# q and k as pairs of 16-bit floats, and P V as one key chunk in every step

## The chip, the core and the metric

The program runs on one core of a Trainium2 chip. The metric is the device time of one execution in microseconds. The kernel before was run three times: 1413.3, 1413.76 and 1414.07 us, so its median is 1413.76 us.

TensorE does the matrix products, VectorE, ScalarE and GpSimd the work on elements, and SyncE issues most of the transfers. Each of them has its own queue of instructions that it works through in order.

## The reference

An attention layer is followed by a top-1 mixture of experts:

```python
q_pool = q.reshape(B, H, S // 2, 2, D).mean(axis=3)          # 8 x 8 heads, 1152 -> 576 queries, D = 64
scores = scale * np.matmul(q_pool, k.transpose(0, 1, 3, 2))  # 576 x 1152 of each head
scores = scores - np.max(scores, axis=-1, keepdims=True)
attn = np.exp(scores)
attn = attn / (np.sum(attn, axis=-1, keepdims=True) + 1e-09)
attn_out = np.matmul(attn, v)
# then for each of 4608 tokens: one of 8 experts, relu(x W1) W2, times a gate
```

All inputs are float32, and the result is held to float32 accuracy. So the kernel splits each operand into a high and a low part and multiplies the parts.

## The kernel before

The attention works on 32 pairs of heads, one after the other. A pair has 18 steps: 9 chunks of 128 keys for the first head, then 9 for the second. In each step (`scores`, L349 to L390) TensorE makes the scores of one chunk of 128 keys against all 576 queries: two matmuls of 288 columns with the stacked high and low parts of q (L361) and two with the low part of k and a row of maxima (L363). The operands are float32 values of reduced precision (`F32R`): `ka` holds the high part of k twice, `kb` the low part and a row of -1, `qa` the high and low parts of q, `qb` the high part of q and the row maxima. The scores land in one of two tiles of PSUM, `sps0` for the even steps and `sps1` for the odd ones.

Then the weights P = exp(scores) are split into `ph` and `pl`, both of 16 bits. In the steps listed in `PLP` (the odd steps 1 to 15) ScalarE writes `ph` (L377), writes the exact exponential back over the scores in PSUM (L378), and VectorE takes the difference (L381); only then is the score tile free for the step after the next. In all other steps ScalarE writes the exponential to memory (L385) and as `ph` (L386), which frees the score tile, and GpSimd takes the difference (L387). The last pair does the same with other steps (`PLPL`).

Beside this, TensorE makes the scores of the next pair with queries on the partitions (L300: three tiles of 384 columns for every two steps, two of them in an odd step and one in an even one, with one or two matmuls each), and VectorE reduces each to a maximum (L301). After nine rows of them a small transpose, a subtraction (L340) and a transfer put the maxima into `qb`. P V (`av`, L396 to L419) takes one chunk of 128 keys at a time: 5 blocks of queries times three matmuls of 64 or 65 columns (L402 to L404), 15 in all. `BURST` says how many chunks are taken in which step, counted from 6 steps after the scores: two in nearly each even step, none in an odd one. After nine chunks the rows are normalised on VectorE (L411 to L413). A router on the finished heads (L452 to L464 and on) adds a few transposes and small matmuls in even steps.

The operands of a pair are made some 30 steps ahead by the entries of the table `PREP`: two transfers bring q and k; ScalarE casts k to its high part in two halves (`kh`, L227) and q (`qh`, L236); GpSimd adds the two queries of a pooled pair (`qsum`, L233) and makes the low parts of k (`kl`, L230) and q (`ql`, L239); transfers from memory to memory (`dmaf`, L126) lay the parts out in `ka`, `kb`, `qa`, `qb`. v has `lv`, `vh` (L259), `vs` (L263) and `vl` (L266). The order of the instructions on TensorE, VectorE, ScalarE and GpSimd is the order of the code. In each step that is: the differences left from the step before, the routers, the scores and their exponentials, `PREP`, the tiles of maxima, `BURST`, `PREP`.

After the attention come the experts, whose weights (`raw1a`, `raw2a`, `raw1b`, `raw2b`) are loaded by SyncE into memory that the attention's tiles had held: the pools of both stages are laid over each other from the same address on.

## Time and profile before

| | us |
|---|---|
| median of three runs | 1413.76 |
| the profiled execution | 1414.16 |
| its span, first to last instruction | 1412.4 |
| scores of step 0 to those of the last step | about 25 to 925 |

The profiled execution took 1414.16 us, of which 1412.4 us lie between its first and its last instruction. All times below are microseconds from the start of the span unless they are marked ns. A group of instructions is given with its count, its busy time, the mean of one in ns, and the idle time of the engine just before them with what ended it. Matmuls are pipelined: a row of one lasts from its start until its last result is there, so the distance of two starts tells what one costs in a row of many, and the duration of the last one tells when the results can be read. The same holds for ScalarE and VectorE, where the next instruction starts some 0.1 us before the one ahead of it has ended.

### The profile page before, as it was taken

The numbers are of one execution on the slowest core, as the hardware profiler recorded it, in microseconds if no ns is written. First come the engines' busy times: TensorE is split into PE (matmuls) and PEld (weight loads), VectorE is DVE, ScalarE is ACT, GpSimd is POOL, SyncE is SP. The second block draws the span as 40 slices with busy tenths as digits, with TensorE's granted clock in tenths as the row PEclk, the third lists the DMA queues.
The fourth block names the chain that finished last, engine by engine and source line by source line (L and its number), as shares of the span: only waits on it lengthen the run. The fifth ranks groups of instructions, "written<-read, shape, count | busy, mean of one in ns | idle before, by whom it ended". The sixth has DMA issues, their size and how long they took to land.

```text
span 1412.4 us, 38742 instructions
## 1 busy us (share of the span) xinstructions
PE 1345.4 (95%) x15024; PEld 1210.1 (86%) x15024; DVE 1080.5 (77%) x2153; ACT 1088.4 (77%) x1906; POOL 919.6 (65%) x768
## 2 busy tenths in 40 slices
...
PEclk9999999999999999999999999999999999999999
...
GB/s 180 163 191 206 145 186 175 165 169 172 178 157 174 168 178 185 140 176 203 163 137 203 139 191 112 154 170 259 325 241 226 294 239 278 235 280 225 322 240 47
...
## 3 DMA queue, kind: packets, MB, share of 16 engines
...
q8 instruction: 122, 2.00, 0.6%
...
q14 instruction: 69, 0.57, 0.1%
HBM read 169.47 MB, written 22.50 MB: 136 GB/s over the span
## 4 chain that ended last, share of the span: by engine, by line
PE 65%; DVE 18%; ACT 9%; issue 5%; DMA 1%; POOL 1%; ACTq 0%; DVEq 0%; POOLq 0%; SPq 0%
PE hps L918 14%; PE sps L361 10%; PE mp L300 7%; PE sps L363 7%; DVE pl L381 7%; DVE pm L301 5%; PE yp L972 4%; PE yp L973 4%; PE yp L975 4%; ACT sps L378 3%; PE av L402 3%; PE av L404 3%; PE av L403 3%; ACT ph L377 2%; DVE xb L413 1%
## 5 line engine op out<-in xcount | busy, mean ns | idle before, releaser
L301 DVE TENSOR_REDUCE pm<-mp 128x1 f32<-128x384 f32 x864 | 450.5, 550 | 146.6 <-PE mp L300 146.6
L387 POOL TENSOR_TENSOR pl<-p,ph 128x576 f16<-128x576 f32 x324 | 415.4, 1286 | 152.0 <-ACT ph L386 108.1
L361 PE MATMUL sps<-qa,ka 128*128 128x288 f32 x1152 | 282.4, 326 | 34.3 <-DVE pl L381 27.6
L402 PE MATMUL av<-vt,ph 128*128 128x65 f16 x2880 | 295.9, 194 | 0.0
L403 PE MATMUL av<-vt,ph 128*128 128x64 f16 x2880 | 293.9, 194 | 0.0
L404 PE MATMUL av<-vt,pl 128*128 128x65 f16 x2880 | 293.0, 192 | 0.0
L402 PEld LDWEIGHTS <-ph 128*128 128x128 f16 x2880 | 262.5, 97 | 28.2 <-issue 5.0
L300 PE MATMUL mp<-ka,qa 128*128 128x384 f32 x960 | 270.0, 345 | 2.0 <-DVE pm L301 1.7
L403 PEld LDWEIGHTS <-ph 128*128 128x128 f16 x2880 | 265.7, 97 | 0.7
L404 PEld LDWEIGHTS <-pl 128*128 128x128 f16 x2880 | 266.1, 99 | 0.0
L363 PE MATMUL sps<-qb,kb 65*128 65x288 f32 x1152 | 247.5, 297 | 0.0
L385 ACT ACTIVATE p<-sps 128x576 f32<-128x576 f32 x324 | 211.4, 653 | 33.2 <-PE sps L363 32.3
L377 ACT ACTIVATE ph<-sps 128x576 f16<-128x576 f32 x248 | 162.4, 655 | 96.7 <-PE sps L363 82.7
L361 PEld LDWEIGHTS sps<-qa,ka 128*128 128x128 f32 x1152 | 182.3, 190 | 49.7 <-PE av L404 25.2
L381 DVE TENSOR_TENSOR pl<-sps,ph 128x576 f16<-128x576 f32 x248 | 187.9, 758 | 35.8 <-ACT sps L378 30.6
L386 ACT ACTIVATE ph<-sps 128x576 f16<-128x576 f32 x324 | 211.7, 654 | 0.0
L918 PE MATMUL hps<-x,w1h 128*128 128x512 f32 (+1 forms) x608 | 201.5, 391 | 5.4 <-DVE x L899 5.2
L363 PEld LDWEIGHTS sps<-qb,kb 65*128 65x128 f32 x1152 | 187.0, 190 | 0.0
L300 PEld LDWEIGHTS mp<-ka,qa 128*128 128x128 f32 x960 | 163.6, 189 | 13.3 <-DVE pm L301 12.8
L378 ACT ACTIVATE sps<-sps 128x576 f32<-128x576 f32 x248 | 161.7, 652 | 0.0
L918 PE MATMUL hps<-x,w1l 128*128 128x256 f32 (+1 forms) x608 | 143.6, 277 | 0.0
L945 ACT COPY hs<-hps 128x512 f32<-128x512 f32 (+1 forms) x76 | 43.0, 565 | 128.1 <-PE hps L918 120.4
...
## 6 DMA issues: line engine op xcount, KB each, us to landing
...
```

The source lines that it names most:

```text
L300: nc.tensor.matmul(mp, lhsT=l, rhs=r, start=j == 0, stop=j == len(ops) - 1)
L301: nc.vector.tensor_reduce(out=pm[:, i:i + 1], in_=mp, axis=AX.X, op=ALU.max)
L361: nc.tensor.matmul(sps[:, j, 0:288], lhsT=ka[:, h, ks], rhs=qa[:, o + 288 * j:o + 288 * j + 288], start=True, stop=False)
L363: nc.tensor.matmul(sps[:, j, 0:288], lhsT=kb[:, h, ks], rhs=qb[:, h, 288 * j:288 * j + 288], start=False, stop=True)
L381: nc.vector.tensor_tensor(out=pl.rearrange("p (j n) -> p j n", j=2), in0=x, in1=ph2, op=ALU.subtract)
L385: nc.scalar.activation(out=p32.rearrange("p (j n) -> p j n", j=2), in_=x, func=AF.Exp, scale=1.0 / 16)
L386: e_ = nc.scalar.activation(out=ph2, in_=x, func=AF.Exp, scale=1.0 / 16)
L387: nc.gpsimd.tensor_tensor(out=pl, in0=p32, in1=ph, op=ALU.subtract)
L402: nc.tensor.matmul(av_[:, qb, 0:65], lhsT=hi, rhs=vt[:, h, c, 0:65], start=c == 0 and qb == 0, stop=False)
L403: nc.tensor.matmul(av_[:, qb, 0:64], lhsT=hi, rhs=vt[:, h, c, 66:130], start=False, stop=False)
L404: nc.tensor.matmul(av_[:, qb, 0:65], lhsT=lo, rhs=vt[:, h, c, 0:65], start=False, stop=c == NC - 1 and qb == 4)
L918: d['mm'] = nc.tensor.matmul(hp[:, f, 0:n], lhsT=W1[l][g][:, c, fs], rhs=d['x'][:, c, 0:n], start=c == 0 and l == 0, stop=c == 3 and l == 0)
```

## The change

The parts of q and k become 16-bit floats (`F16`), so that the tiles `ka`, `kb`, `qa`, `qb`, `kp`, `xk`, `xq`, `yq` have half the bytes. k is multiplied by 4096 before it is split, on ScalarE as the scale of the cast (`kh` is now an ACTIVATE), and on GpSimd by a new instruction `ks` ahead of `kl`; the exponentials divide by 4096 again through their scale. The row of -1 becomes -32768, and the row maxima are divided by 32768. `qs` gets a tile of its own. In `PREP` the entry `ks` stands at 17 and `kl` moves from 18 to 20. `BURST` becomes one chunk in each of the 18 steps. `PLP` gets the step 17.

```diff
-PREP = ((0, 'lk'), (12, 'kh', 0), (12, 'qsum'), (17, 'kh', 1), (18, 'kl'), (18, 'dk', 0), ...
+PREP = ((0, 'lk'), (12, 'kh', 0), (12, 'qsum'), (17, 'kh', 1), (17, 'ks'), (20, 'kl'), (18, 'dk', 0), ...
-BURST = {0: 2, 2: 2, 4: 2, 6: 2, 8: 1, 10: 2, 12: 2, 14: 2, 16: 3}
-PLP = (1, 3, 5, 7, 9, 11, 13, 15)
+BURST = {i: 1 for i in range(18)}
+PLP = (1, 3, 5, 7, 9, 11, 13, 15, 17)
+KS, KR = 2.0 ** 12, 2.0 ** 15
...
-                L[i] = (lp if i == order[2] else ep).tile(shape, F32R, name=f"{name}{i}")
+                L[i] = (lp if i == order[2] else ep).tile(shape, F16, name=f"{name}{i}")
...
-        nc.vector.memset(KBs[0].bitcast(F32)[64:65], -1.0)
+        nc.vector.memset(KBs[0][64:65], -KR)
...
             def kh(i):
                 z = slice(i * NQ, i * NQ + NQ)
-                nc.scalar.copy(out=xk[:, z], in_=kpf[:, z])
+                nc.scalar.activation(out=xk[:, z], in_=kpf[:, z], func=AF.Copy, scale=KS)
+
+            def ks():
+                nc.gpsimd.tensor_scalar(out=kpf, in0=kpf, scalar1=KS, scalar2=1.0, op0=ALU.mult, op1=ALU.mult)
 
             def kl():
-                nc.gpsimd.tensor_tensor(out=kp, in0=kpf, in1=xk.bitcast(F32), op=ALU.subtract)
+                nc.gpsimd.tensor_tensor(out=kp, in0=kpf, in1=xk, op=ALU.subtract)
...
-                    nc.vector.tensor_scalar(out=mr, in0=tp, scalar1=c0, scalar2=None, op0=ALU.subtract)
+                    nc.vector.tensor_scalar(out=mr, in0=tp, scalar1=c0, scalar2=1.0 / KR, op0=ALU.subtract, op1=ALU.mult)
...
-                    nc.scalar.activation(out=ph2, in_=x, func=AF.Exp, scale=1.0 / 16)
-                    e_ = nc.scalar.activation(out=x, in_=x, func=AF.Exp, scale=1.0 / 16)
+                    nc.scalar.activation(out=ph2, in_=x, func=AF.Exp, scale=1.0 / 16 / KS)
+                    e_ = nc.scalar.activation(out=x, in_=x, func=AF.Exp, scale=1.0 / 16 / KS)
```

TensorE, an odd step of pair 11 and what follows it, before (`sps11` the scores, `mp12` the tiles of maxima of the next pair, `tp` a transpose of the router, `av11` P V):

```order
L361 MATMUL sps11_7444<-qa2_125,ka2_122 128x288 x2
L363 MATMUL sps11_7444<-qb2_128,kb2_119 128x288 x2
L300 MATMUL mp12_7454<-ka0_123,qa0_126 128x384
L300 MATMUL mp12_7459<-ka0_123,qa0_126 128x384
L452 MATMUL tp_7463<-ident_64,xb_5498 128x128 x2
L361 MATMUL sps11_7469<-qa2_125,ka2_122 128x288 x2
L363 MATMUL sps11_7469<-qb2_128,kb2_119 128x288 x2
L300 MATMUL mp12_7478<-ka0_123,qa0_126 128x384 x2
L402 LDWEIGHTS ph_7249
L402 MATMUL av11_7410<-vt1_137,ph_7249 128x65
```

The same place now, from the last matmul of the odd step's scores on (line numbers are 4 higher):

```order
L367 LDWEIGHTS kb2_119
L367 MATMUL sps11_7445<-qb2_128,kb2_119 128x288
L304 LDWEIGHTS qa0_126
L304 MATMUL mp12_7454<-ka0_123,qa0_126 128x384
L304 LDWEIGHTS qa0_126
L304 MATMUL mp12_7459<-ka0_123,qa0_126 128x384
L406 LDWEIGHTS ph_7238
L406 MATMUL av11_7424<-vt1_137,ph_7238 128x65
L407 LDWEIGHTS ph_7238
L407 MATMUL av11_7424<-vt1_137,ph_7238 128x64
L408 LDWEIGHTS pl_7239
L408 MATMUL av11_7424<-vt1_137,pl_7239 128x65
```

Fifteen matmuls of P V have moved between the odd step's tiles of maxima and the scores of the even step, and each matmul on 16-bit operands has a weight load as an instruction of its own.

VectorE, from the difference of step 15 of pair 11 to that of step 1 of pair 12, before (`pl` the difference, `pm` the maxima of one tile, `m9` those of a row):

```order
L381 TENSOR_TENSOR pl_7717<-sps11_7718,ph_7716 128x576
L301 TENSOR_REDUCE pm_7555<-mp12_7744 128x1
L301 TENSOR_REDUCE pm_7555<-mp12_7789 128x1
L301 TENSOR_REDUCE pm_7555<-mp12_7792 128x1
L308 TENSOR_REDUCE m9_7795<-pm_7555 128x4
L301 TENSOR_REDUCE pm_7809<-mp13_7810 128x1
L301 TENSOR_REDUCE pm_7809<-mp13_7861 128x1
L301 TENSOR_REDUCE pm_7809<-mp13_7864 128x1
L381 TENSOR_TENSOR pl_7844<-sps12_7845,ph_7843 128x576
```

And now:

```order
L385 TENSOR_TENSOR pl_7733<-sps11_7734,ph_7732 128x576
L305 TENSOR_REDUCE pm_7571<-mp12_7776 128x1
L305 TENSOR_REDUCE pm_7571<-mp12_7803 128x1
L305 TENSOR_REDUCE pm_7571<-mp12_7806 128x1
L385 TENSOR_TENSOR pl_7795<-sps11_7796,ph_7794 128x576
L312 TENSOR_REDUCE m9_7809<-pm_7571 128x4
L305 TENSOR_REDUCE pm_7839<-mp13_7840 128x1
L305 TENSOR_REDUCE pm_7839<-mp13_7877 128x1
L305 TENSOR_REDUCE pm_7839<-mp13_7880 128x1
L385 TENSOR_TENSOR pl_7859<-sps12_7860,ph_7858 128x576
```

A ninth difference, that of step 17, stands on VectorE in each pair, and GpSimd has one fewer.

GpSimd, where the operands of pair 13 are made during pair 11, before (`kp13` the low part of k, `yq` the sum and then the low part of q):

```order
L233 TENSOR_TENSOR yq_7238<-qp_7235 128x576
L387 TENSOR_TENSOR pl_7397<-p32_7403,ph_7396 128x576
L230 TENSOR_TENSOR kp13_7233<-kpf_7234,xk13_7237 128x1152
L387 TENSOR_TENSOR pl_7468<-p32_7474,ph_7467 128x576
L239 TENSOR_TENSOR yq_7238<-yq_7238,xq_7239 128x576
```

And now:

```order
L237 TENSOR_TENSOR qs_7252<-qp_7249 128x576
L391 TENSOR_TENSOR pl_7411<-p32_7417,ph_7410 128x576
L231 TENSOR_SCALAR kpf_7248<-kpf_7248 128x1152
L234 TENSOR_TENSOR kp13_7247<-kpf_7248,xk13_7251 128x1152
L391 TENSOR_TENSOR pl_7484<-p32_7490,ph_7483 128x576
L243 TENSOR_TENSOR yq_7253<-qs_7252,xq_7254 128x576
```

The multiplication of k stands directly ahead of the subtraction, so two long instructions follow each other on GpSimd. On ScalarE the order of the instructions is the same as before.

## Rows read from the trace of the kernel before

**Rows 1.** The page: busy time of each engine, and the granted clock of TensorE over 40 slices of the span.

```profile
PE 1345.4 (95%) x15024; PEld 1210.1 (86%) x15024; DVE 1080.5 (77%) x2153; ACT 1088.4 (77%) x1906; POOL 919.6 (65%) x768
...
PEclk9999999999999999999999999999999999999999
```

**Rows 2.** Busy time of each engine in stretches of the span: stretch, length, busy time and instructions of PE, PEld, DVE, ACT and POOL, then granted clock, share of the transfer engines, GB/s.

```profile
500.00:600.00 100.00, 95.84 (x1403) 88.95 (x1402) 78.94 (x183) 85.06 (x155) 83.04 (x68) 1.00 0.61 165
...
1000.00:1050.00 50.00, 50.00 (x263) 42.60 (x262) 42.63 (x80) 29.31 (x42) 14.14 (x13) 1.00 0.72 255
```

**Rows 3.** Groups of instructions in the 400 us from 300 to 700, shapes kept apart.

```profile
L387 POOL TENSOR_TENSOR pl<-p,ph 128x576 f16<-128x576 f32 x143 | 183.4, 1286 | 62.3 <-ACT ph L386 43.3 <-PE mp L300 13.4 <-DVE pm L301 3.5
L361 PE MATMUL sps<-qa,ka 128*128 128x288 f32 x514 | 125.2, 325 | 15.3 <-DVE pl L381 12.7 <-DVE lA L475 1.6 <-DVE lA L473 1.0
L404 PEld LDWEIGHTS <-pl 128*128 128x128 f16 x1276 | 117.5, 99 | 0.0
L361 PEld LDWEIGHTS sps<-qa,ka 128*128 128x128 f32 x514 | 81.1, 189 | 21.6 <-PE av L404 12.4 <-issue 8.0 <-ACT ph L386 0.8
L377 ACT ACTIVATE ph<-sps 128x576 f16<-128x576 f32 x114 | 74.7, 655 | 41.4 <-PE sps L363 35.7 <-PE mp L300 2.5 <-POOL pl L387 1.4
L230 POOL TENSOR_TENSOR kp<-kpf,xk 128x1152 fp32r<-128x1152 f32 x14 | 37.3, 2662 | 0.0
L263 POOL TENSOR_SCALAR vp<-vp 128x576 f32<-128x576 f32 x30 | 20.2, 673 | 2.5
```

**Rows 4.** The timeline of one loop of the odd score tile, from the scores of step 1 of a pair to the exponential of step 3: start, length, engine, line, operation.

```profile
560.89 0.51 PE L361 MATMUL sps<-qa,ka 128*128 128x288 f32 x2
561.24 0.43 PE L363 MATMUL sps<-qb,kb 65*128 65x288 f32 x2
561.51 0.51 PE L300 MATMUL mp<-ka,qa 128*128 128x384 f32 x2
561.76 0.65 ACT L377 ACTIVATE ph<-sps 128x576 f16<-128x576 f32 x1 [0.38 <-PE sps L363]
...
562.12 0.43 PE L363 MATMUL sps<-qb,kb 65*128 65x288 f32 x2
562.31 0.65 ACT L378 ACTIVATE sps<-sps 128x576 f32<-128x576 f32 x1
...
563.06 0.76 DVE L381 TENSOR_TENSOR pl<-sps,ph 128x576 f16<-128x576 f32 x1 [0.16 <-ACT sps L378]
...
563.96 0.50 PE L361 MATMUL sps<-qa,ka 128*128 128x288 f32 x2 [0.21 <-DVE pl L381]
...
564.83 0.65 ACT L377 ACTIVATE ph<-sps 128x576 f16<-128x576 f32 x1 [0.77 <-PE sps L363]
```

**Rows 5.** The timeline of ScalarE in another pair: the first exponentials (L377) of the odd steps 5, 7, 9, 11, 13 and 15, with the two casts of k between the first two and the cast of v between the steps 11 and 13.

```profile
595.66 0.65 ACT L377 ACTIVATE ph<-sps 128x576 f16<-128x576 f32 x1 [0.77 <-PE sps L363]
...
596.77 0.66 ACT L227 CAST xk<-kpf 128x576 fp32r<-128x576 f32 x1
...
598.40 0.68 ACT L227 CAST xk<-kpf 128x576 fp32r<-128x576 f32 x1
598.97 0.67 ACT L377 ACTIVATE ph<-sps 128x576 f16<-128x576 f32 x1
...
602.05 0.65 ACT L377 ACTIVATE ph<-sps 128x576 f16<-128x576 f32 x1
...
605.32 0.65 ACT L377 ACTIVATE ph<-sps 128x576 f16<-128x576 f32 x1 [0.57 <-PE sps L363]
...
606.43 1.15 ACT L259 ACTIVATE vt<-vp 128x1152 f16<-128x1152 f32 x1
...
608.55 0.66 ACT L377 ACTIVATE ph<-sps 128x576 f16<-128x576 f32 x1
...
611.62 0.65 ACT L377 ACTIVATE ph<-sps 128x576 f16<-128x576 f32 x1 [0.47 <-PE sps L363]
```

**Rows 6.** The timeline of ScalarE at the end of the pair ahead of that of rows 4: the first exponentials of the steps 15 and 17.

```profile
556.10 0.65 ACT L377 ACTIVATE ph<-sps 128x576 f16<-128x576 f32 x1 [0.48 <-PE sps L363]
...
559.10 0.65 ACT L385 ACTIVATE p<-sps 128x576 f32<-128x576 f32 x1 [0.70 <-PE sps L363]
```

**Rows 7.** The timeline of TensorE over the last scores ahead of a burst of P V and the first and the last of its 30 matmuls.

```profile
603.36 0.33 PE L300 MATMUL mp<-ka,qa 128*128 128x384 f32 x1
603.53 0.20 PE L402 MATMUL av<-vt,ph 128*128 128x65 f16 x1
...
604.43 0.19 PE L404 MATMUL av<-vt,pl 128*128 128x65 f16 x1
```

**Rows 8.** The end of the attention: transfers issued by SyncE, and casts of the weights on ScalarE.

```profile
905.25 0.94 SPq L847 DMA_DIRECT2D raw2a<-in_w_dram  x2
925.08 1.19 SPq L845 DMA_DIRECT2D raw1b<-in_w_dram  x2
926.56 1.33 SPq L847 DMA_DIRECT2D raw2b<-in_w_dram  x2
...
943.77 1.05 ACT L879 CAST w2h<-raw2a 128x1024 fp32r<-128x1024 f32 x1
...
947.53 1.05 ACT L873 CAST w1h<-raw1b 128x1024 fp32r<-128x1024 f32 x1
...
954.31 1.05 ACT L879 CAST w2h<-raw2b 128x1024 fp32r<-128x1024 f32 x1 [0.81 <-PE yp L975]
```

More of the change, by code (lines that the diff above doesn't have):

```diff
@@ L125, in dmaf @@
         def dmaf(o, i, q=nc.sync):
-            return q.dma_start(out=o.bitcast(F32), in_=i.bitcast(F32))
+            return q.dma_start(out=o, in_=i)
         lastv = [None]
@@ L136, in prep @@
             states[n] = dict(ka=ka, kb=kb, qa=qa, qb=qb, vt=vt, p=p, n=n)
-            kp = ld.tile([128, S], F32R, name=f"kp{n}", tag="kp", bufs=KPB)
+            kp = ld.tile([128, S], F16, name=f"kp{n}", tag="kp", bufs=KPB)
             kpf = ld.tile([128, S], F32, name="kpf")
@@ L140, in prep @@
             vp = ld.tile([128, 2 * NC, 64], F32, name="vp")
-            xk = sq.tile([128, S], F32R, name=f"xk{n}", tag="xk")
-            yq = sq.tile([128, NQ], F32R, name="yq")
-            qs = yq.bitcast(F32)
-            xq = sq.tile([128, NQ], F32R, name="xq")
+            xk = sq.tile([128, S], F16, name=f"xk{n}", tag="xk")
+            qs = sq.tile([128, NQ], F32, name="qs")
+            yq = sq.tile([128, NQ], F16, name="yq")
+            xq = sq.tile([128, NQ], F16, name="xq")
             def lk():
@@ L161, in fsel @@
             def fsel():
-                x = p3.tile([128, NQ], F32R, name="sel", tag="p32", bufs=P32)
+                x = p3.tile([128, 2 * NQ], F16, name="sel", tag="p32", bufs=P32)
                 for h in range(2):
@@ L167, in fsel @@
                     nc.gpsimd.tensor_copy(out=x[:, o + 64:o + 128], in_=i_)
-                    nc.gpsimd.memset(x.bitcast(F32)[:, o + 128:o + 192], 0.0)
+                    nc.gpsimd.memset(x[:, o + 128:o + 192], 0.0)
                     nc.gpsimd.tensor_copy(out=x[:, o + 192:o + 256], in_=i_)
@@ L175, in qsv @@
                 nc.vector.tensor_copy(out=xq, in_=qp[:, 0])
-                nc.vector.tensor_tensor(out=yq, in0=qp[:, 0], in1=xq.bitcast(F32), op=ALU.subtract)
+                nc.vector.tensor_tensor(out=yq, in0=qp[:, 0], in1=xq, op=ALU.subtract)
             def klh(i):
                 z = slice(i * NQ, i * NQ + NQ)
-                nc.vector.tensor_tensor(out=kp[:, z], in0=kpf[:, z], in1=xk.bitcast(F32)[:, z], op=ALU.subtract)
+                nc.vector.scalar_tensor_tensor(out=kp[:, z], in0=kpf[:, z], scalar=KS, in1=xk[:, z], op0=ALU.mult, op1=ALU.subtract)
             def shift(ops):
@@ L238, in ql @@
             def ql():
-                nc.gpsimd.tensor_tensor(out=yq, in0=qs, in1=xq.bitcast(F32), op=ALU.subtract)
+                nc.gpsimd.tensor_tensor(out=yq, in0=qs, in1=xq, op=ALU.subtract)
             def dk(h):
@@ L268, in prep @@
             P = functools.partial
[L269 removed]
+            fns = dict(lf=lf, fsel=fsel, qsv=qsv, klh=klh, sk=sk, sl=sl, sq0=sq0, sq1=sq1, lk=lk, ks=ks, lv=lv, kh=kh, kl=kl, qsum=qsum, qh=qh, ql=ql, dk=dk, dq=dq, dl=dl, vh=vh, vs=vs, vl=vl)
             out = {}
@@ L335, in rows @@
                 nc.tensor.transpose(out=tp, in_=m9[:, 0:nt], identity=ident)
-                mr = sm.tile([5, 128], F32R, name="mr")[0:nt]
-                c0 = 16.0 * SHIFT
+                mr = sm.tile([5, 128], F16, name="mr")[0:nt]
+                c0 = 16.0 * KS * SHIFT
                 def split(tp=tp, tk=tk, mr=mr, qbf=qbf, t0=t0, t1=t1, nt=nt):
-                    nc.vector.tensor_scalar(out=mr, in0=tp, scalar1=c0, scalar2=None, op0=ALU.subtract)
+                    nc.vector.tensor_scalar(out=mr, in0=tp, scalar1=c0, scalar2=1.0 / KR, op0=ALU.subtract, op1=ALU.mult)
                     free(tk)
@@ L366, in scores @@
                 if c + 9 * h in PLPL and st['n'] == LASTN:
-                    nc.scalar.activation(out=ph2, in_=x, func=AF.Exp, scale=1.0 / 16)
+                    nc.scalar.activation(out=ph2, in_=x, func=AF.Exp, scale=1.0 / 16 / KS)
                     for j in range(2):
                         px, pk = psum(True, "px")
-                        e_ = nc.scalar.activation(out=px[:, 0:288], in_=x[:, j], func=AF.Exp, scale=1.0 / 16)
+                        e_ = nc.scalar.activation(out=px[:, 0:288], in_=x[:, j], func=AF.Exp, scale=1.0 / 16 / KS)
                         def lo(px=px, pk=pk, j=j, ph2=ph2, pl=pl):
```

11 lines of the change are left out of this document (5 added, 6 removed).

## The prediction

> **What bounds the kernel now.** I read the page first. TensorE is called busy for 95% of the span at the full clock [rows 1], but a row of a matmul lasts until its last result is there, so in rows that overlap this share says little. Next come the stretches: in the attention, as from 500 to 600, TensorE shows 96, ScalarE 85, GpSimd 83 and VectorE 79 of 100 us [rows 2]. Nobody is full and all are close, so the question is which loop of waits sets the step. The groups give the rate: 143 steps with the difference on GpSimd and 114 with it on VectorE in 400 us [rows 3], 1.556 us a step, 3.11 for two, 28.0 for a pair of heads. Among the idle times, ScalarE waits 41 of the 400 us ahead of an odd exponential, mostly for L363, and TensorE 15 ahead of L361, mostly for VectorE's difference [rows 3]. These two waits belong to one loop, and the timeline shows it closed [rows 4]: the odd scores start at 560.89 and end at 561.24 + 0.43 = 561.67; exponentials from 561.76 to 562.31 + 0.65 = 562.96; VectorE's difference from 563.06 to 563.82; the next odd scores at 563.96. That is 3.07 us with only hand-overs of 0.09, 0.10 and 0.14 in it. No step of it waits for anything else, so this loop is the floor of two steps: the odd score tile has one buffer, and is free only after the difference.
>
> Over a pair the odd exponentials stand 3.31 (steps 5 to 7), 3.08 (7 to 9), 3.27 (9 to 11), 3.23 (11 to 13) and 3.07 (13 to 15) apart [rows 5], 559.10 - 556.10 = 3.00 from 15 to 17, and 561.76 - 559.10 = 2.66 from 17 to 1 [rows 4, 6]; the two cycles from 1 to 5 I take at the floor, 3.07. Sum 27.76. Two kinds lie above the floor. From 5 to 9 and 11 to 13 ScalarE has its own work: between the exponentials at 595.66 and 598.97 two casts of k follow the others without a gap [rows 5]. From 9 to 11 ScalarE waits for scores instead (the mark of 0.57 at 605.32): TensorE came late, with transposes and a burst of 30 ahead. The one cycle below the floor, 17 to 1, has no difference on VectorE in it.
>
> **16-bit operands, matmul by matmul.** Four matmuls of 288 columns take 0.78 us from the first start to the last end. The last starts at 561.24 + (0.43 - 0.295) = 561.375, so the three distances are 0.485 together; two L300 of 384 columns stand 0.51 - 0.34 = 0.17 apart [rows 4]. The nearest 16-bit rows are P V: 29 distances in 604.43 - 603.53 = 0.90 us, 0.031 each, for 65 columns with a weight load before every one [rows 7]. At 2.4 GHz (the granted clock is 1.00 [rows 2]) 65 columns are 0.027, which leaves 0.004 over. So 288 columns in 16 bits: 0.120 + 0.004 = 0.124, three of them 0.37; 384 columns 0.164. A weight load is 99 ns instead of 189 [rows 3], which is why the first distance after a pause, the dearest now, should lose most. The last matmul lasts 0.19 - 0.027 + 0.120 = 0.28. So 0.37 + 0.28 = 0.65 to 0.66 instead of 0.78: the loop loses 0.12 and becomes 2.95. Bounds: 0.78 (no gain, if what is over the 0.120 is not the load) and, with the return from VectorE to TensorE shorter by up to 0.1 because the load is, a loop of 2.85. I take 2.95, from the 16-bit row.
>
> The row of P V stands 0.031 apart, load and matmul. The Trainium skill (TensorE: Matmul & The Clock Gate, section Back-to-back issue gap) gives more for a stream of loads and matmuls in a real kernel, about 81 ns at 128 columns, some 28 over the columns. By it 288 columns would be 0.148 apart and the loop about 3.02, a third of the gain lost; rows 7 do not bear it out.
>
> **P V in every step.** Thirty matmuls in two steps before and after, so no work is gained; what moves is when TensorE is free. Counted from the start of the odd scores, TensorE now has scores (4 x 0.124 = 0.50), two tiles of maxima (0.33), 15 of P V (0.46), even scores (0.50), a tile (0.16, or 0.33 when it takes two matmuls), P V (0.46): 2.4 to 2.6, and 0.3 more with three transposes, against 2.80 at which VectorE frees the odd tile. So TensorE is no longer late, and the cycle 9 to 11 falls to 2.95. In return the even scores come later: they start at 1.28 and end at 1.94, whereas before they ended 562.12 + 0.43 - 560.89 = 1.66 after [rows 4]. ScalarE starts the odd exponentials at 561.76 - 560.89 - 0.12 = 0.75 and is done with issuing them 1.10 later, at 1.85, so it idles about 0.18. In a cycle at the floor that costs nothing (4 x 0.55 + 0.18 = 2.38 of 2.95). In the cycles that ScalarE fills, casts stand in that place (the first cast of k and that of v come right behind the odd exponentials [rows 5]) or ScalarE is already late. I cost it at nothing; without that cover it is 0.2 to 0.35 in each of three cycles.
>
> **The ninth difference on VectorE.** Cycle 17 to 1 becomes a loop like the others: 2.95 instead of 2.66, a loss of 0.29 a pair. VectorE gains 0.76 a pair beside a share of 79 in 100; GpSimd loses 1.29.
>
> **k times a constant.** On ScalarE the cast keeps its shape and place: 0.66 to 0.68 now, 0.65 for the exponentials of the same size [rows 5], so nothing. On GpSimd `ks` is twice the 576 elements of L263, 2 x 0.673 = 1.35; `kl` stays at 2.66 or falls to twice L387, 2.57 [rows 3]. With one difference fewer, GpSimd is level to 0.1 a pair. `ks` and `kl` in a row block its queue for 4.0 us instead of 2.66, with a difference of `pl` behind them; that one is read by P V six steps, some 9 us, later. Hidden; if that cover went, up to 1.3 a pair. The transfers from `xk`, `xq`, `yq`, `kp` halve; nobody is seen waiting for them, so nothing.
>
> **The experts.** Their tiles now lie over others: the halved tiles of the last pair come to lie under the second half of `raw2a`, whose load was issued at 905.25 and must now wait for the last scores, around 924, and `raw1b`, `raw2b` stand behind it on SyncE. That is 1 MB more ahead of them, 4 us at 255 GB/s [rows 2]. `raw1b`, issued at 925.08, is first cast at 947.53, `raw2b` at 954.31, the second half of `raw2a` at 943.77 [rows 8]: 2 to 4 MB need 8 to 16 us, so each is there in time by some 8 us. Nothing, at worst 4.
>
> **Sum.** A pair afterwards: six cycles at 2.95 (1 to 5, 9 to 11, 13 to 17, 17 to 1 makes 2 + 1 + 2 + 1) and 3.31 + 3.08 + 3.23, which ScalarE sets as before: 17.70 + 9.62 = 27.32, a gain of 0.44. The mean pair is 28.0, 0.24 above this quiet one; about half of that is TensorE being late, and goes: 0.12. For 30 pairs 0.56 x 30 = 17 us. The first and the last pair I leave. The profiled execution took 1414.2, 0.4 above the median of the three runs: 1414.2 - 17 - 0.4 = 1397.
>
> **The rivals.** *More*: the return shortens to a loop of 2.85, and all of the mean pair's lateness goes: 6 x 2.85 + 9.62 = 26.7 against 28.0, 39 us at most, 1375; I put the case at 1382. For it speaks the weight load's halving; against it that the hand-overs to ScalarE and VectorE, which load no weights, are 0.09 and 0.10 too [rows 4]. *No change*: the F16 distances stay as they are. Then the six cycles are 3.07 with 17 to 1 dearer by 0.41 and 9 to 11 cheaper by 0.2: 0.2 a pair lost, 0.12 of lateness won, 1414 to 1416. For it: TensorE streams 288 columns in about the same time in either format. *Slower*: ScalarE becomes the bound. The even scores come 0.35 later behind P V, and in a cycle in which ScalarE has over 0.55 of other work behind the even exponentials this wait is not covered. If it is paid in all three filled cycles at 0.35 it is 1.05 a pair, less 0.56: 0.5 x 30 = 15 us, 1429; paid in two, about 1419. It decides from the point where the cast of q or the second cast of k no longer finds ScalarE late. Against it: 595.66 to 602.05 is one row without a gap, so even scores have 0.3 to spare there [rows 5].
>
> **How the numbers follow.** The forecast 0.57 (its own range 1390 to 1406), more 0.20, no change 0.11, slower 0.12. The range 1381 to 1413 leaves out the far end of more and the slower case. A change of 0.2%, 2.8 us, is about what a measurement of this kernel can tell from none. Faster: 0.57 + 0.20 + 0.02 of no change = 0.79; same 0.09; slower 0.12.
>
> **What would show it.** In the changed profile the four L365 and L367 of a step should last 0.65 to 0.66 us, not 0.78; odd exponentials in quiet cycles should be 2.95 apart, and 2.95 from 17 to 1; ScalarE should run without a gap from 5 to 9, and 3.3 and 3.1 should stay there; TensorE's idle time ahead of the odd scores should be longer than now and end with VectorE's difference. I am wrong if ScalarE's idle time ahead of the even exponentials (L389) appears in cycles of over 3.1, if P V waits for GpSimd, or if the experts start later than the attention ends.

## The result and the profile after

The changed kernel took 1420.97 us (median of seven runs, 1417.67 to 1429.21) where the kernel before took 1413.3 us in seven runs beside it: a ratio of 1.0066 with a 95% interval of 1.0042 to 1.0091. It is slower, by 7.7 us on the medians and 9 by the ratio; 1397 was forecast. The profiled execution took 1418.95 us, its span is 1417.2 us. The experiments below ran on several chips; each ratio is to the kernel before on the same chip (its medians lay between 1409.97 and 1415.46 us), so times of different rounds are best compared by their ratios. One execution of `e_early`, of 1460.01 us at a mean granted clock of 0.848, was in the slow state and is left out of its figures.

The page of the changed kernel, engines and granted clock:

```profile
PE 1288.4 (91%) x15024; PEld 1052.1 (74%) x15024; DVE 1101.5 (78%) x2184; ACT 1103.5 (78%) x1906; POOL 902.1 (64%) x768
...
PEclk9999999999999999999999999999999999999999
```

Beside [rows 1] TensorE is busy 57 us less, its weight loads 158 us less, and yet the span is longer. One stretch of the attention, columns as in [rows 2]:

```profile
500.00:600.00 100.00, 88.21 (x1377) 70.35 (x1377) 81.54 (x186) 86.60 (x153) 80.35 (x66) 1.00 0.45 122
```

TensorE fell from 96 to 88 of 100 us, nobody else became full: something waits. The groups from 300 to 700 (as [rows 3]) say where:

```profile
L406 PE MATMUL av<-vt,ph 128*128 128x65 f16 x1280 | 142.9, 193 | 31.0 <-DVE xb L417 31.0
...
L365 PE MATMUL sps<-qa,ka 128*128 128x288 f16 x512 | 105.5, 287 | 10.6 <-DVE pl L385 10.5
...
L385 DVE TENSOR_TENSOR pl<-sps,ph 128x576 f16<-128x576 f32 x128 | 96.8, 756 | 26.2 <-ACT sps L382 24.8 <-POOL pl L391 1.0 <-POOL kpf L231 0.3
L389 ACT ACTIVATE p<-sps 128x576 f32<-128x576 f32 x129 | 83.7, 649 | 16.6 <-PE sps L367 15.6
L381 ACT ACTIVATE ph<-sps 128x576 f16<-128x576 f32 x128 | 83.7, 654 | 31.7 <-PE sps L367 29.5
...
L365 PEld LDWEIGHTS <-ka 128*128 128x128 f16 x512 | 35.5, 101 | 17.5 <-DVE pl L385 15.3
L234 POOL TENSOR_TENSOR kp<-kpf,xk 128x1152 f16<-128x1152 f32 x14 | 33.2, 2374 | 1.2
...
L231 POOL TENSOR_SCALAR kpf<-kpf 128x1152 f32<-128x1152 f32 x14 | 16.1, 1151 | 1.2
```

The first line is new: ahead of P V (L406) TensorE stands idle for 31.0 of 400 us and waits for `xb` of L417, the last instruction of the normalisation. Before, the same line was:

```profile
L402 PE MATMUL av<-vt,ph 128*128 128x65 f16 x1277 | 130.7, 194 | 0.0
```

The loads of the scores' weights fell from 189 to 101 ns. ScalarE's wait ahead of the odd exponentials (L381) fell from 41 to 32 us.

The timeline of one quiet loop of the odd score tile in the changed kernel, steps 1 to 3 of a pair (as [rows 4]):

```profile
477.16 0.42 PE L365 MATMUL sps<-qa,ka 128*128 128x288 f16 x2 [0.32 <-DVE pl L385]
...
477.42 0.41 PE L367 MATMUL sps<-qb,kb 65*128 65x288 f16 x2
...
477.92 0.65 ACT L381 ACTIVATE ph<-sps 128x576 f16<-128x576 f32 x1 [0.47 <-PE sps L367]
...
478.47 0.65 ACT L382 ACTIVATE sps<-sps 128x576 f32<-128x576 f32 x1
...
479.22 0.76 DVE L385 TENSOR_TENSOR pl<-sps,ph 128x576 f16<-128x576 f32 x1 [0.17 <-ACT sps L382]
...
480.04 0.42 PE L365 MATMUL sps<-qa,ka 128*128 128x288 f16 x2 [0.20 <-DVE pl L385]
...
480.80 0.65 ACT L381 ACTIVATE ph<-sps 128x576 f16<-128x576 f32 x1 [0.47 <-PE sps L367]
```

Scores 0.67 us (477.16 to 477.83), and 0.06 from the end of the difference (479.98) to the next scores: 2.88 for 3.07 before. The faster loop came. Two loops later in the same pair, from step 5 to step 7, stands what ate it:

```profile
483.67 0.65 ACT L381 ACTIVATE ph<-sps 128x576 f16<-128x576 f32 x1 [0.47 <-PE sps L367]
...
484.69 0.33 PE L304 MATMUL mp<-ka,qa 128*128 128x384 f16 x1
...
484.97 0.76 DVE L385 TENSOR_TENSOR pl<-sps,ph 128x576 f16<-128x576 f32 x1 [0.17 <-ACT sps L382]
...
485.64 0.15 DVE L415 TENSOR_SCALAR rs<-av 128x5 f32<-128x5 f32 x1
485.83 0.19 DVE L416 RECIPROCAL rs<-rs 128x5 f32<-128x5 f32 x1
...
486.05 0.49 DVE L417 TENSOR_TENSOR xb<-av,rs 128x320 f32<-128x320 f32 x1
...
486.60 0.20 PE L406 MATMUL av<-vt,ph 128*128 128x65 f16 x1 [1.59 <-DVE xb L417]
...
487.07 0.41 PE L365 MATMUL sps<-qa,ka 128*128 128x288 f16 x2
...
487.82 0.65 ACT L381 ACTIVATE ph<-sps 128x576 f16<-128x576 f32 x1 [0.71 <-PE sps L367]
```

P V has one accumulator, the tile `av` (a pool of one buffer). The last chunk of a pair's second head is now taken in step 5. Its normalisation comes in step 6, on VectorE behind the difference of score tile 5 (L385), and the first chunk of the next head is put into TensorE's queue in the same step 6. TensorE works in order: from 485.02 to 486.60 it waits for the accumulator, and the scores of step 7, whose tile is free at 485.73, stand behind it until 487.07. The old `BURST` took the last three chunks in step 4, none in step 5, and the next head's first two in step 6: a whole step in which VectorE could normalise.

The length of each loop of the odd score tile, worked out from the starts of the odd scores (L361, L365) and averaged over pairs 3 to 30 without 26 and 27, in which the set-up of the experts stands in the queues too (and, from 17 to 1, without pair 30, which the last pair follows), in us; the other columns are the experiments below without the `e_` of their names (f32 new is `e_f32_newburst`):

| loop | before | after | oldburst | normfirst | early | f32 new | f32 new, norm | no17 | no15 | no1 | vlate |
|---|---|---|---|---|---|---|---|---|---|---|---|
| 1 to 3 | 3.07 | 2.87 | 2.94 | 2.87 | 2.87 | 3.07 | 3.07 | 2.88 | 2.87 | 2.50 | 2.87 |
| 3 to 5 | 3.13 | 2.87 | 2.90 | 2.87 | 2.94 | 3.07 | 3.07 | 2.87 | 2.81 | 2.86 | 2.87 |
| 5 to 7 | 3.17 | **4.43** | 2.97 | 3.43 | 2.94 | **4.49** | 3.54 | 3.43 | 3.42 | 3.43 | 3.43 |
| 7 to 9 | 3.40 | 2.97 | 3.42 | 2.99 | 3.31 | 3.37 | 3.19 | 3.00 | 2.99 | 2.94 | 2.99 |
| 9 to 11 | 3.27 | 3.13 | 3.05 | 3.13 | 3.10 | 3.31 | 3.31 | 3.13 | 3.30 | 3.45 | 3.13 |
| 11 to 13 | 3.14 | 2.95 | 2.96 | 2.95 | 2.94 | 3.24 | 3.24 | 2.95 | 2.95 | 2.96 | 2.95 |
| 13 to 15 | 3.18 | 3.17 | 3.29 | 3.16 | 3.17 | 3.37 | 3.37 | 3.15 | 3.15 | 3.15 | 3.06 |
| 15 to 17 | 3.06 | 2.98 | 2.99 | 2.98 | 3.12 | 3.07 | 3.07 | 2.99 | 2.97 | 2.98 | 3.09 |
| 17 to 1 | 2.65 | 2.89 | 2.89 | 2.89 | 2.89 | 2.69 | 2.68 | 2.39 | 2.38 | 2.39 | 3.22 |
| pair | 28.07 | 28.27 | 27.41 | 27.28 | 27.27 | 29.68 | 28.55 | 26.79 | 26.86 | 26.66 | 27.61 |

In before and after the attention ends at the same time (last first exponential at 925.1 and 924.7; the first pair and pair 26, in which the experts are set up, were each 3 us shorter, and that made up for the rest). Behind it lie 1412.4 - 925.1 = 487.3 us before and 1417.2 - 924.7 = 492.5 now: 5.2 us more in the stage of the experts. What SyncE issued there in the changed kernel, the first cast of `raw1b`, and two stretches:

```profile
924.47 0.94 SPq L851 DMA_DIRECT2D raw2a<-in_w_dram  x2
925.60 0.37 SPq L849 DMA_DIRECT2D raw1b<-in_w_dram  x1
942.06 0.37 SPq L551 DMA_DIRECT2D xrows<-xb  x1
942.47 0.52 SPq L552 DMA_DIRECT2D xrows<-xb  x1
943.18 1.19 SPq L849 DMA_DIRECT2D raw1b<-in_w_dram  x1
944.57 1.95 SPq L851 DMA_DIRECT2D raw2b<-in_w_dram  x2
```

```profile
955.62 1.04 ACT L877 CAST w1h<-raw1b 128x1024 fp32r<-128x1024 f32 x1 [4.35 <-DMA raw1b<-in_w_dram]
```

```profile
930.00:935.00 5.00, 2.55 (x16) 1.90 (x16) 2.41 (x12) 2.93 (x6) 2.00 (x1) 0.94 0.87 340
935.00:940.00 5.00, 4.59 (x15) 3.98 (x15) 0.06 (x1) 2.10 (x3) 5.00 (x4) 0.50 0.01 5
```

The second of the stretches before:

```profile
935.00:940.00 5.00, 4.93 (x34) 4.04 (x32) 3.41 (x17) 2.66 (x4) 2.79 (x2) 1.00 0.67 245
```

The loads that stood together from 905.25 to 926.56 [rows 8] are now torn apart: `raw2a` at 924.47, half of `raw1b` and `raw2b` behind the stores of the last rows (942.06). TensorE, half idle from 930 to 935, runs at 1.2 GHz (0.50) from 935 to 940, where before it stood at 1.00. The second expert tile starts (ScalarE's first copy of its sums, `hs`) 46.7 us behind the last exponential, 38.3 before.

### The profile page after: what moved, and what is told of

Read it like the earlier page. It is cut to its first block, busy times and chain, and to the rows that moved or that the text cites. A ratio compares the mean times of both kernels' runs of the same rounds, so it can differ in the third digit from the quotient of the medians.

```text
span 1417.2 us, 38144 instructions
## 1 busy us (share of the span) xinstructions
PE 1288.4 (91%) x15024; PEld 1052.1 (74%) x15024; DVE 1101.5 (78%) x2184; ACT 1103.5 (78%) x1906; POOL 902.1 (64%) x768
## 4 chain that ended last, share of the span: by engine, by line
PE 34%; issue 20%; DVE 20%; ACT 13%; POOL 8%; DMA 3%; ACTq 1%; POOLq 0%; DVEq 0%; SPq 0%
DVE pl L385 8%; PE sps L365 6%; ACT sps L382 5%; PE sps L367 5%; DVE pm L305 5%; PE mp L304 5%; ACT ph L381 4%; PE av L406 3%; PE hps L922 3%; PE av L407 3%; PE av L408 3%; POOL out_dram L991 2%; DVE xb L417 2%; POOL ids L717 2%; POOL xg L728 2%
## 5 line engine op out<-in xcount | busy, mean ns | idle before, releaser
L391 POOL TENSOR_TENSOR pl<-p,ph 128x576 f16<-128x576 f32 x293 | 373.8, 1278 | 160.2 <-ACT ph L390 121.5
L406 PE MATMUL av<-vt,ph 128*128 128x65 f16 x2880 | 321.3, 193 | 68.6 <-DVE xb L417 68.6
L406 PEld LDWEIGHTS <-ph 128*128 128x128 f16 x2880 | 267.8, 96 | 122.0 <-DVE xb L417 91.6
L407 PE MATMUL av<-vt,ph 128*128 128x64 f16 x2880 | 321.4, 194 | 0.0
L408 PE MATMUL av<-vt,pl 128*128 128x65 f16 x2880 | 320.6, 192 | 0.0
L365 PE MATMUL sps<-qa,ka 128*128 128x288 f16 x1152 | 237.3, 287 | 28.6 <-DVE pl L385 28.1
L304 PE MATMUL mp<-ka,qa 128*128 128x384 f16 x960 | 254.3, 326 | 2.5 <-DVE pm L305 1.0
L385 DVE TENSOR_TENSOR pl<-sps,ph 128x576 f16<-128x576 f32 x279 | 211.0, 756 | 58.1 <-ACT sps L382 54.2
L381 ACT ACTIVATE ph<-sps 128x576 f16<-128x576 f32 x279 | 182.5, 654 | 75.2 <-PE sps L367 67.2
L367 PE MATMUL sps<-qb,kb 65*128 65x288 f16 x1152 | 236.4, 286 | 0.0
L389 ACT ACTIVATE p<-sps 128x576 f32<-128x576 f32 x293 | 191.1, 652 | 39.5 <-PE sps L367 36.9
L367 PEld LDWEIGHTS <-kb 65*128 65x128 f16 x1152 | 113.2, 98 | 29.1
L976 PE MATMUL yp<-w2h,hh 128*128 128x512 f32 x322 | 128.0, 398 | 3.5 <-ACT hh L953 3.5
L977 PE MATMUL yp<-w2l,hh 128*128 128x512 f32 x322 | 125.8, 391 | 0.0
```

The costliest lines, as they stand in the source:

```text
L304: nc.tensor.matmul(mp, lhsT=l, rhs=r, start=j == 0, stop=j == len(ops) - 1)
L365: nc.tensor.matmul(sps[:, j, 0:288], lhsT=ka[:, h, ks], rhs=qa[:, o + 288 * j:o + 288 * j + 288], start=True, stop=False)
L367: nc.tensor.matmul(sps[:, j, 0:288], lhsT=kb[:, h, ks], rhs=qb[:, h, 288 * j:288 * j + 288], start=False, stop=True)
L381: nc.scalar.activation(out=ph2, in_=x, func=AF.Exp, scale=1.0 / 16 / KS)
L385: nc.vector.tensor_tensor(out=pl.rearrange("p (j n) -> p j n", j=2), in0=x, in1=ph2, op=ALU.subtract)
L391: nc.gpsimd.tensor_tensor(out=pl, in0=p32, in1=ph, op=ALU.subtract)
```

## The experiments

**Taking the stall away, and the two parts of the change apart.** The theory (A): the one accumulator costs some 1.3 us a pair and hides the gain of the faster loop. Rivals: ScalarE is the bound (B, the prediction's slower case), or the loss lies with the experts alone (C).

`e_early`, the last chunk of each head one step earlier:

```diff
-BURST = {i: 1 for i in range(18)}
+BURST = {**{i: 1 for i in range(18)}, 7: 2, 8: 0, 16: 2, 17: 0}
```

> One change to the kernel after: the last chunk of P V of each head is taken one step early, in pairs (BURST has 2 chunks at 7 and none at 8, 2 at 16 and none at 17), so that a step without P V lies between two heads. Theory A (the one P V accumulator: the first P V of a pair waits for the normalisation of the pair before, which stands in VectorE's queue behind the difference of score tile 5): the loop from odd score 5 to odd score 7 falls from 4.43 us to 2.9 to 3.3 us, a quiet pair from 27.8 to 26.3 to 26.7, and 31 such places give 36 to 47 us back: 1374 to 1386 us. Rival B (the prediction's slower case: ScalarE is the bound, because the even scores come later): the place of one chunk changes nothing for the even scores, 1416 to 1422 us. Rival C (the loss is one of the stage of the experts alone): the attention stage keeps its pair of 27.8 us, 1416 to 1422 us.

Measured: 1391.62 us (median of three), a ratio to before of 0.9876 (0.9858 to 0.9895). The loop 5 to 7 is 2.94; but 7 to 9 grew from 2.97 to 3.31, because ScalarE then works without a gap from step 5 to step 9, through the casts of k. A's mechanism holds, but its range (to 1386) is missed, for a third of the gain is taken back. B falls: the even scores start 1.6 us behind the odd ones in this run as in the changed kernel, and the time fell all the same. C falls too: a pair went from 28.27 to 27.27.

`e_normfirst`, the normalisation into VectorE's queue at once:

```diff
-IMM = 0
+IMM = 1
```

> One change to the kernel after: IMM is 1, so that the normalisation (L415 to L417) is put into VectorE's queue as soon as the last P V of a head is issued, ahead of the difference of score tile 5 and not behind it. P V itself stays one chunk in every step. Theory A: what costs is where the normalisation stands, so the loop from 5 to 7 falls from 4.43 us to 3.0 to 3.6 us (the difference itself now stands behind some 0.6 us of normalisation), 25 to 44 us in all: 1377 to 1396 us. A variant of it, A2 (the accumulator needs a whole step between two heads, whatever the order on VectorE): the loop stays above 4 us and the time above 1407 us. Rivals B and C: 1416 to 1422 us.

Measured: 1392.23 us, 0.9876 (0.986 to 0.9892). Its timeline at the same place in a pair:

```profile
468.56 0.65 ACT L381 ACTIVATE ph<-sps 128x576 f16<-128x576 f32 x1 [0.47 <-PE sps L367]
...
469.60 0.15 DVE L415 TENSOR_SCALAR rs<-av 128x5 f32<-128x5 f32 x1
...
470.01 0.49 DVE L417 TENSOR_TENSOR xb<-av,rs 128x320 f32<-128x320 f32 x1
470.41 0.75 DVE L385 TENSOR_TENSOR pl<-sps,ph 128x576 f16<-128x576 f32 x1
...
470.56 0.20 PE L406 MATMUL av<-vt,ph 128*128 128x65 f16 x1 [0.66 <-DVE xb L417]
...
471.21 0.41 PE L365 MATMUL sps<-qa,ka 128*128 128x288 f16 x2
...
471.96 0.65 ACT L381 ACTIVATE ph<-sps 128x576 f16<-128x576 f32 x1
```

The wait ahead of P V is 0.66 instead of 1.59; now the difference comes 0.5 later, behind the normalisation. The loop is 3.43 instead of 4.43. On the mean a pair is 1.0 us shorter: 0.75 in a quiet one, 1.5 in one with a router. So it was the place of three small instructions in VectorE's queue, 0.83 us of work, that cost 1.9% of the time (1.0066 to 0.9876).

`e_f32_newburst`, the kernel before with P V in every step alone, and `e_f32_newburst_norm`, the same with `IMM = 1`:

```diff
-BURST = {0: 2, 2: 2, 4: 2, 6: 2, 8: 1, 10: 2, 12: 2, 14: 2, 16: 3}
+BURST = {i: 1 for i in range(18)}
```

> The kernel before with one part of the change alone: one chunk of P V in every step; q and k stay float32 words with their constant 1, and step 17 keeps its GpSimd difference. Theory A: the stall of 1.2 to 1.5 us at the loop from 5 to 7 comes in full and nothing of the faster scores pays for it, +30 to +47 us: 1443 to 1461 us. Rival B: +5 to +15 us. Rival C, and the prediction's step that P V in every step costs nothing: 1412 to 1416 us.

Measured: 1461.12 us, 1.0372 (1.0347 to 1.0397), 52 us dearer, a little more than A's 30 to 47.

> The kernel before with one chunk of P V in every step and with IMM 1 (the normalisation ahead of the difference of score tile 5): e_f32_newburst with its suspected stall taken away, q and k still float32 words. Theory A: the loop from 5 to 7 falls from 4.49 to 3.3 to 3.5 us and TensorE keeps its full clock in the pairs with a router, so that most of the 51 us of e_f32_newburst go: 1412 to 1430 us. Rival (in every step P V stands in the way of the scores also elsewhere, in the loops 7 to 15, and that is the larger part): 1440 us or more.

Measured: 1429.38 us, 1.0126 (1.0107 to 1.0146): with the normalisation moved, two thirds of the loss are gone. The waits of the weight loads from 300 to 700, waited for, sum, times and longest, in the first and then the second of the two:

```profile
PEld L402 <- DVE xb L413: 31.6, 27, 2.5
```

```profile
PEld L402 <- DVE xb L413: 15.9, 28, 0.8
```

The other third is partly the wait that is left at 5 to 7 (3.54 for 3.17), and partly the loops 9 to 15 (0.04, 0.10 and 0.19 over before). There it is the even scores that come late, behind 15 matmuls of P V: ScalarE's wait for them ahead of the even exponentials has doubled, before and in `e_f32_newburst_norm`, from 300 to 700:

```profile
L385 ACT ACTIVATE p<-sps 128x576 f32<-128x576 f32 x143 | 93.1, 651 | 13.6 <-PE sps L363 13.3
```

```profile
L385 ACT ACTIVATE p<-sps 128x576 f32<-128x576 f32 x140 | 91.0, 650 | 29.5 <-PE sps L363 27.6
```

This is what the prediction's slower case feared, and with float32 words it shows; in the changed kernel the same wait (L389) is 16.6.

`e_oldburst`, the 16-bit floats and the ninth difference with the old `BURST`:

> The kernel after with the BURST table of before (bursts of 30 in the even steps, one odd step without P V between two heads), so the pairs of 16-bit floats and the ninth VectorE difference alone. Theory A: nothing stalls between two heads, the loops between other steps are 2.87 to 3.3 us as in the other runs with 16-bit floats, a quiet pair takes 26.9 to 27.4 us and the kernel 1385 to 1400 us. Rival (the prediction's no-change case, that the faster scores end in ScalarE's queue and gain nothing whatever P V does): 1406 to 1414 us.

Measured: 1396.48 us, 0.9873 (0.9834 to 0.9911): inside A's range. So the 16-bit operands together with the ninth difference are worth 18 us (1.27% of 1413.3), and P V in every step took 27 = 9 + 18 us. The operands alone, in no run by themselves, should be worth more, since the ninth difference costs time (`e_norm_no17`, below). From the table: (27.41 - 28.07) x 30 = -20 and (28.27 - 27.41) x 30 = +26. In the float32 kernel the same `BURST` cost 52. The stall itself does not make the difference: by the table it is 28.27 - 27.28 = 0.99 a pair with 16 bits and 29.68 - 28.55 = 1.13 with float32 words. With the normalisation moved, P V in every step costs the float32 kernel 28.55 - 28.07 = 0.48 a pair, and gains the 16-bit kernel 27.41 - 27.28 = 0.13: there it loses 0.15 in a quiet pair and gains about 1 in one with a router.

**The clock as an amplifier.** In every fourth pair, where a router's work stands in the queues too, TensorE waits up to 2.5 us at the same place. In two such pairs of the changed kernel, the stretch up to that wait's end and the one behind it:

```profile
172.68:175.68 3.00, 0.85 (x8) 0.38 (x4) 2.20 (x9) 3.00 (x6) 2.82 (x3) 1.00 0.00 0
...
176.68:179.68 3.00, 3.00 (x26) 2.14 (x24) 1.88 (x5) 1.43 (x3) 2.83 (x3) 0.50 0.87 201
```

```profile
286.73:289.73 3.00, 0.86 (x8) 0.39 (x4) 2.20 (x9) 3.00 (x6) 2.81 (x3) 1.00 0.01 3
...
290.73:293.73 3.00, 2.97 (x46) 2.36 (x45) 2.18 (x7) 2.33 (x5) 2.83 (x3) 1.00 0.86 201
```

Almost the same idle time, and once the clock halves and once it does not; the pair that meets it takes 30.49 instead of 29.1 us. In `e_f32_newburst` five such pairs took 31.5 us and two 30.1; in `e_f32_newburst_norm` all take 28.7 to 28.8. With the stall these falls go too.

**What bounds the attention next.** `e_norm_vlate`, `e_normfirst` with v's preparation three to four steps later (`vh` from 84 to 96, that is by four, the rest by three):

> e_normfirst with the five pieces of v's preparation later by some four steps (vh from 84 to 96 and so on), so that the cast of v on ScalarE (1.15 us) falls behind step 15, where ScalarE waits 0.46 us for scores, and no longer behind step 11, where it has worked without a gap since step 5. Theory (with the stall gone, the next bound of a pair is ScalarE's stretch without a gap in the steps 5 to 13): the loop from 13 to 15 falls from 3.16 to 2.9 us, a pair by 0.15 to 0.4 us, the time to 1380 to 1388 us. Rival (VectorE's loop of 2.87 us is the bound throughout, and ScalarE's casts only fill its gaps): 1390 to 1394 us.

Measured: 1401.37 us, 0.992 (0.9892 to 0.9947): the wrong way. 13 to 15 fell by 0.1 as expected, but 15 to 17 and 17 to 1 grew by 0.1 and 0.33: the cast of 1.15 us does not fit into a gap of 0.46. ScalarE has gaps in the steps 15 to 3, but none that holds the whole cast.

`e_norm_no17`, `e_normfirst` without the ninth VectorE difference:

```diff
-PLP = (1, 3, 5, 7, 9, 11, 13, 15, 17)
+PLP = (1, 3, 5, 7, 9, 11, 13, 15)
```

> e_normfirst without the ninth VectorE difference: step 17 keeps its GpSimd difference, as before the change. The prediction priced that difference at 0.29 us a pair (the loop from 17 to 1 from 2.66 to 2.95). If so: the loop falls from 2.89 to 2.5 to 2.66 us, and the time from 1392 to 1383 to 1386 us. Rival (the gain at 17 is taken back within the next steps, because ScalarE or GpSimd is late there): 1389 to 1395 us.

Measured: 1391.01 us, 0.9833 (0.9793 to 0.9872). The loop 17 to 1 fell by 0.50 and the attention ends at 884.6 instead of 896.7. But in this profile the stage of the experts takes 505.4 us instead of 493.8, so the ratio shows only half of it (0.9876 to 0.9833); the other three runs, at mean granted clocks of 0.984 to 0.989 where those of `e_normfirst` had 0.990 to 0.993, seem to share this. In `e_norm_no17_pad`, below, with the same loops, the whole of it shows.

`e_norm_no15` and `e_norm_no1` also drop the difference of step 15 or of step 1:

```diff
-PLP = (1, 3, 5, 7, 9, 11, 13, 15)
+PLP = (1, 3, 5, 7, 9, 11, 13)
```

```diff
-PLP = (1, 3, 5, 7, 9, 11, 13, 15)
+PLP = (3, 5, 7, 9, 11, 13, 15)
```

> e_norm_no17 with one VectorE difference less again: step 15 too goes through GpSimd (PLP is 1 to 13). If the loop of the odd score tile over VectorE is the bound of the steps 15 to 3 (2.87 us for 2.39 us over GpSimd): the loop from 15 to 17 falls from 2.98 to 2.4 to 2.7 us, a pair by 0.3 to 0.5 us, 9 to 15 us off e_norm_no17. Rival (GpSimd, busy 85% of the time, is then late with its differences and P V waits for them): a loop further on grows by as much, and the time is within 4 us of e_norm_no17 or above it.

Measured: 1378.61 us, 0.9772 (0.9751 to 0.9792). The loop 15 to 17 did not fall (2.97): without the difference the next scores just come 1.08 us after the tile is free, and 9 to 11 grew by 0.17. A pair is as long as in `e_norm_no17` (26.86 for 26.79), so the rival's price holds; the median is lower because in this profile the stage of the experts took some 13 us less than in that of `e_norm_no17`. The rival's mechanism is another: no P V waits for GpSimd. What waits is ScalarE's cast of q, for GpSimd's sum of q, in every fourth pair (from 300 to 700: sum, times, longest; in `e_norm_no17` it does not wait):

```profile
ACT xq L240 <- POOL qs L237: 2.9, 4, 0.7
```

> As e_norm_no15, but it is step 1 that goes through GpSimd beside step 17, and step 15 keeps VectorE: two GpSimd differences more in a row (0, 1, 2 and 16, 17). Theory of the loop over VectorE: the loop from 1 to 3 falls from 2.87 to 2.4 to 2.7 us, 6 to 15 us off e_norm_no17. Rival of the late GpSimd: within 4 us of e_norm_no17 or above it, with waits for GpSimd's pl ahead of P V.

Measured: 1371.43 us, 0.9735 (0.9706 to 0.9764), the lowest, but a second set of runs of the same code, below, gave 0.9782. The loop 1 to 3 fell by 0.38, and 9 to 11 grew by 0.32, for the most part at the same cast:

```profile
ACT xq L240 <- POOL qs L237: 3.7, 4, 1.0
```

So by the table only 0.13 a pair is left; each theory saw a part.

**The stage of the experts.** `e_pad` puts an unused tile of the same size behind each of the attention's q and k tiles, so that the experts' tiles lie over the attention's as before; `e_norm_pad`, `e_norm_no17_pad` and `e_norm_no1_pad` do the same to the kernels of those names, and `e_norm_no1_again` is the partner of the last.

```diff
-                L[i] = (lp if i == order[2] else ep).tile(shape, F16, name=f"{name}{i}")
+                q = lp if i == order[2] else ep
+                L[i] = q.tile(shape, F16, name=f"{name}{i}")
+                q.tile(shape, F16, name=f"pad_{name}{i}")
```

> One change to the kernel after: behind each of the attention's four q and k tiles lies an unused one of the same size, so that the experts' tiles lie over the attention's where they lay before. The arithmetic and the order of the attention are those of after. Theory A with its second part (5 us are lost where the experts begin, because their second transfer of weights lies over tiles that the last pair still reads, and a store of xrows stands on SyncE between the transfers): raw2a is issued by 906 us, the second half of raw1b by 928 us, and the time falls by 3 to 7 us, to 1414 to 1418 us. Rival (the layout costs nothing, and the 5 us come from the casts or the clock): 1419 to 1422 us. The attention stage keeps its loop of 4.43 us by both.

Measured: 1418.79 us, 1.0063 (1.0042 to 1.0084), no gain that shows. The transfers stand together again (`raw2a` at 908.48, the rest of `raw1b` at 927.99), and the second tile starts 41.1 us behind the last exponential instead of 46.7. But TensorE still drops to the half clock there, the end lies 489.9 behind instead of 492.5, and in this profile four of the pairs with a router took 30.3 to 30.5 us instead of one.

> e_normfirst with the unused tiles of e_pad, so that the experts' tiles lie where they lay before. In e_pad the stretch behind the last exponential took 2.6 us less than in after (489.9 for 492.5 us), and TensorE still fell to the half clock there. Theory (place of the tiles 2.6 us, clock the other 2.6 us): 1388 to 1391.5 us, the stretch behind the last exponential 490 to 492 us. Rival (the difference in e_pad was chance): 1391.5 to 1394 us, 493 us or more behind the last exponential.

Measured: 1393.61 us, 0.9859 (0.9826 to 0.9892), 492.5 us behind the last exponential: the time is the rival's, the stretch lies between the two.

> e_norm_no17 with the unused tiles of e_pad. By the loops the attention ends where that of e_norm_no17 did (884.6 us); the second expert tile starts 41 to 43 us behind the last exponential in place of 45.6 us, as in e_pad and e_norm_pad. If the place of the tiles is worth these 3 to 5 us in the end: a ratio to before of 0.978 to 0.982; if later pauses of TensorE in the stage of the experts take it back, as the profile of e_norm_pad has it: 0.982 to 0.985.

Measured: 1376.26 us, 0.9755 (0.9736 to 0.9775); second tile at 42.7 us, 492.0 us behind the last exponential. That is below both ranges; it is 0.0104 under `e_norm_pad`, 15 us, as much as the 0.49 a pair of the ninth difference makes in 30 pairs.

> The same code as e_norm_no1, run once more as the partner of e_norm_no1_pad on one chip. A ratio to before of 0.971 to 0.976, the second expert tile 45 to 46 us behind the last exponential.

Measured: 1380.88 us, 0.9782 (0.9755 to 0.9809); second tile at 45.7 us, 492.4 behind the last exponential. That is 9 us over the first run of the same code on another chip, and above the range.

> e_norm_no1 with the unused tiles of e_pad behind the attention's q and k tiles: the loops of the attention stay as in its partner, only the experts' tiles lie where they lay before. Theory (the place of the tiles costs the changed kernel 3 to 5 us where the experts begin, and this is still there at the end): 3 to 5 us under e_norm_no1_again. Rival (the experts' later transfers take most of it back, as the profiles of e_norm_pad and e_norm_no17_pad have it): within 2 us of it.

Measured: 1373.99 us, 0.9747 (0.972 to 0.9775); second tile at 41.4 us, 492.0 behind. The medians differ by 7 us, but in the two profiles the stages behind the attention by 0.4; the rest is in pairs 26 and 27 (33.76 + 32.22 and 32.44 + 29.02 us), which the tiles have no part in. The lead of 4 us is still there at 386 us behind the last exponential and nearly gone (0.8) at 410. So the place of the tiles makes the second tile 3 to 6 us later, for which every pair of runs agrees (even with the old place it is at 41 to 43 us, not at 38.3); whether that is worth anything at the end stays open. `e_f32_newburst_norm`, with the old place and its second tile at 41.3 us, ends at 492.0 too, so most of the 5 us cannot be put down to the place alone.

## Why the prediction was wrong

The step that failed is "**P V in every step**": "no work is gained; what moves is when TensorE is free ... I cost it at nothing". It followed TensorE's work through a loop in the middle of a head and looked at the even scores, and it never asked what the first P V of the next head waits for. Over 30 pairs it costs the 26 us above. Without it, `e_oldburst` and `e_normfirst` lie 18 us under before, where the forecast (17 us) put the whole change, but that is partly luck: in the profile of `e_normfirst` the attention ends 28 us earlier (896.7 for 925.1) and the stage of the experts takes 6.5 us more (493.8 for 487.3), where the forecast had 17 and nothing.

- **Operands.** Right, but for the return edge. The four matmuls last 0.67 for 0.65 to 0.66; the three distances are 477.42 + (0.41 - 0.285) - 477.16 = 0.385 together, 0.128 each for 0.124. The return edge did shorten, from 0.14 to 0.06, so the loop is 2.87, near the bound of 2.85, not the 2.95 taken. The Trainium skill (TensorE: Matmul & The Clock Gate, Back-to-back issue gap) gives about 81 ns at 128 columns and about 131 ns at 512. The prediction carried the first figure alone to 288 columns and so came to 148 ns; an estimate on the straight line between the page's two figures would be 102 ns. This trace's 128 ns agrees with neither.
- **The ninth difference.** 17 to 1 is 2.89 for 2.95. But its price was reckoned against the old 2.66; in the new kernel the loop without it is 2.39, so it costs 0.50 a pair, not 0.29.
- **Loops that ScalarE fills.** In a quiet pair of `e_normfirst` the odd exponentials stand 3.41 (5 to 7), 3.11 (7 to 9) and 3.22 (11 to 13) apart for the forecast 3.31, 3.08 and 3.23, and the other six 2.87 to 2.90 for 2.95 (in some quiet pairs 3.02 from 15 to 17): 27.0 to 27.15 for 27.32. In the changed kernel 5 to 7 is 4.15 in such a pair; the rest of the sum holds. (Counted by scores, as in the table, ScalarE's lateness shows one loop later.)
- **The slower rival.** The sign was right and the mechanism wrong. ScalarE's wait ahead of the even exponentials (L389) is 16.6 us in 400, against 31.0 of TensorE ahead of P V, and both cures leave the even scores as late as they are. Its premise held: the even scores start 1.60 us behind the odd ones on the mean, 1.18 before. But its price was small: of those 16.6 us, 13.6 were there before. Two signs that the prediction named did not come: TensorE's idle time ahead of the scores was to grow and fell from 15.3 to 10.6 us (L361, L365), and ScalarE was to run without a gap from 5 to 9 and waits 0.71 us ahead of step 7.
- **k times a constant.** Hidden, as costed (no P V waits for GpSimd in the trace), and cheaper: `ks` 1.15 and `kl` 2.37, 3.52 together for the 4.0 reckoned.
- **The experts.** "Nothing, at worst 4" was 5.2 in the profile. The load of `raw2a` at 924.47 stood where the text put it ("around 924"). What it missed is that the stores of `xrows` come between the loads on SyncE (942.06), so that `raw1b` is first cast at 955.62 instead of 947.53, and that TensorE's clock falls to 0.50 behind its pause. How much of the 5.2 us either makes stays open.
